# FFN and value products read their tokens alternately from two halves of a tile: pooled attention, ELU FFN and squared-ReLU FFN on one core

## The chip, the core and the metric

The kernel runs on one core of a Trainium2 chip. The metric is the device time of one execution in microseconds; the profile and its trace come from one profiled execution. PE is TensorE's matmul engine and PEld its weight loads, DVE is VectorE, ACT is ScalarE, POOL is GpSimd, and SP issues most DMAs.

## What is computed

With float32 in and out, for 2 batches of 12288 queries of 128 channels (24576 tokens in all):

```
kv_pool = kv.reshape(B, H/4, 4, W/4, 4, C).mean(axis=(2, 4))      # 768 keys per batch
k = v = kv_pool.reshape(B, 768, C) @ w_sr
a = softmax(q @ k.T / sqrt(C));   x = a @ v                       # 24576 x 128
h = x @ w_in1  (128 -> 2048);     g = where(h > 0, h, exp(min(h, 0)) - 1);   y = g @ w_out1
h = relu(y @ w_in2);              out = (h * h) @ w_out2          # 24576 x 128
```

## The kernel before

**Tiles.** Tokens go in 48 blocks `t` of 512; channels or FFN features lie on the 128 partitions, tokens along the free dimension, in every stage from the attention's values on. An FFN has 16 chunks `i` of 128 features. For each block, the attention makes scores for four groups of 128 queries (L688 to L690), row maximum, exponential, normalisation, and turned probabilities; a move by DMA finishes their transposition, and `values` (L806 to L811) makes x with tokens in the columns. Blocks 0 to 2 (`EARLY`, `PLAIN`) make their values in another way, at L833, by full fp32 matmuls.

**Products in parts.** For accuracy each float32 operand is kept as a high and a low part in fp32r (names end in H and L), and `products` (L306 to L310) makes three matmuls of one: low weight by high data, high weight by high data, high weight by low data. Each has 128 weights columns and a moving operand of 512 columns, one PSUM bank. So a block has 16 `hidden` products for each FFN (L875), 16 `down` products for each (L942), and 6 of values: 70 products of three matmuls, 210 in all, and 24 matmuls for the scores (half with 512 columns, half with 256). The last block's `down` of the second FFN runs in two halves of 256 tokens.

**Between the products.** For the ELU (`elu`, L884): `exp` on ACT, `less_one` on POOL, `pick` on DVE (tile `g`), then per pair of chunks `aH` on ACT (tile `gH`) and `aL` on DVE (tile `gL`). For the squared ReLU (`relu2`, L917): `relu` and `square` on ACT (tile `r`), `aH` on POOL (tile `sH`), `aL` on DVE (tile `sL`). `split` makes the two parts of x and y from PSUM. `store` (L965) transposes the result in 32 x 32 squares on DVE (tile `o`) and writes it with four DMAs, one for each 32 channels.

**What sets the order.** Every operation is entered in a `Program` with its engine, a cost in ns, a due time, what it comes after, and the buffers that it takes. `Program.order` (L92) runs a model of the five engines once, when the kernel is built: each engine takes the ready operation that is due first, with a little patience. Costs are multiplied by a factor `SLACK` per engine after the first 130 us. A table `MOVED` shifts the due times of single operations by hand, most of them in the opening (keys `(chunk)` or `(FFN, block, chunk)`). The result is one fixed order on each engine; every engine then works through its own in order and waits on semaphores. In the opening, PE is kept busy with matmuls on an identity (`fill`).

Of the kernel before, what the change touches and what calls it, by code (L numbers as in the profile page):

```python
# [22 lines left out]
IDLE, MARGIN, FILLER, COLD, WARM = 330.0, 60.0, 224.0, 430.0, 6300.0  # L23
OPENING, EAGER = 60000.0, 250.0
BULK = 130000.0
SLACK = {"pe": 1.0, "act": 1.17, "dve": 1.1, "pool": 1.16, "sp": 1.0}
LATENCY = {"pe": 197, "act": 135, "dve": 110, "pool": 120, "sp": 2300}
SAME = {"pe": 0, "act": 110, "dve": 0, "pool": 60, "sp": 2300}
BEGIN = {"pe": 1360.0, "act": 2500.0, "dve": 900.0, "pool": 1300.0, "sp": 1800.0}

MOVED = {
    "aH": {(0, 0, 3): 3720, (0, 2, 6): 28360, (1, 1, 5): 1580},
    "aL": {(0, 2, 2): 200, (0, 3, 1): 22430, (1, 1, 3): 2340},
    "cut": {(0, 0, 1): 12280, (0, 1, 1): 18660, (1, 1, 3): 17420},
    "down": {(0, 0, 10): -7210, (0, 0, 11): -61170, (0, 0, 9): -390, (0, 1, 11): 1860, (0, 2, 3): 17140,
        (0, 2, 9): 14060, (0, 3, 0): 4990, (0, 3, 8): -7760, (1, 0, 0): -34230, (1, 0, 11): 8280, (1, 0, 2): -28660,
        (1, 1, 2): 360, (1, 1, 3): -12810},
    "exp": {(0, 5): 9510, (0, 6): 7700, (1, 14): 10480, (2, 1): 1790, (3, 12): 55960, (3, 13): 8500},
    "hidden": {(0, 0, 12): -20, (0, 0, 8): 6730, (0, 1, 13): -3490, (0, 1, 15): -360, (0, 1, 6): 7080,
# [6 lines left out]
    "high_part": {(0, 1, 0): 11700, (1, 1, 2): 20980, (1, 1, 3): 9580},  # L46
    "join": {(1, 0, 2): -10420, (1, 1, 3): -28280},
    "k_hi": {(0, 1): -90},
    "less_one": {(3, 10): -10910, (3, 14): 17140},
    "low_part": {(1, 0, 1): 18510},  # L50
    "normalise": {(3, 0): 520, (4, 2): 4360},
    "pick": {(1, 11): 12410, (2, 0): 18920, (2, 3): -14380, (2, 6): -13180, (3, 10): -8840},
    "q_transpose": {(2,): -3420},
    "recip": {(3, 3): -2180},
    "relu": {(0, 3): -10730, (0, 7): -410, (1, 15): 11630, (1, 6): -29110, (2, 8): -3270},
    "scores": {(3, 1): 4220, (4, 3): -3470},
    "turn": {(4, 1): 11280},
    "v_hi": {(0,): 24340},
    "values": {(1, 3): -13460, (2, 1): 18540, (2, 3): 7470, (3, 2): 15850},
    "xL": {(3,): -2040},  # L60
    "yH": {(3,): -19030},
}


class Program:
# [18 lines left out]
    def op(self, name, engine, cost, priority, fn, after=(), takes=(), last=(), port=False):  # L84
        assert name not in self.ops, name
        if port:
            self.port.add(name)
        self.ops[name] = (engine, cost, priority, fn, tuple(after), tuple(takes))
        for key in last:
            self.readers.setdefault(key, set()).add(name)  # L90

    def order(self, kinds, fill=None):  # L92

        for tag, moved in MOVED.items():
            for key, by in moved.items():
                engine, cost, priority, *rest = self.ops[(tag, *key)]
                self.ops[(tag, *key)] = (engine, cost, priority + by, *rest)
# [77 lines left out]
def kernel(  # L175
# [19 lines left out]
    nc = tc.nc  # L195
# [104 lines left out]
    def buf(*key):  # L300
        return live[key]

    def f32(t):
        return t.bitcast(F32)

    def products(dst, lhs, rhs, start=True, stop=True):  # L306

        nc.tensor.matmul(dst, lhs[1], rhs[0], start=start, stop=False)  # L308
        nc.tensor.matmul(dst, lhs[0], rhs[0], start=False, stop=False)  # L309
        nc.tensor.matmul(dst, lhs[0], rhs[1], start=False, stop=stop)  # L310
# [295 lines left out]
    G = P // 32  # L606
    q_rows = q.rearrange("b (t g j) c -> (b t) j g c", g=NB // 32, j=32)
    q_tokens = q.rearrange("b (t s p) c -> (b t) p s c", s=NS, p=P)
    out_rows = out.rearrange("(t g j) c -> t j g c", g=NB // 32, j=32)

    def pieces(x, a):
        return x[32 * a:32 * (a + 1), :].rearrange("p (g i) -> p g i", i=32)
# [11 lines left out]
    def parts(tag, *t):  # L624
        return buf(tag + "H", *t), buf(tag + "L", *t)

    def attention(t, base):
# [168 lines left out]
        def weigh(j, due):  # L796
            k = (t, j)
            c0 = slice(2 * j, 2 * j + 2)

            def p_hi():  # L800
                nc.scalar.copy(buf("pH", t)[:, c0, :], f32(buf("pL", t))[:, c0, :])

            def p_lo():
                x = buf("pL", t)[:, c0, :]
                nc.vector.tensor_sub(x, f32(x), f32(buf("pH", t)[:, c0, :]))

            def values():
                vH, vL = buf("vH", b), buf("vL", b)
                for i in range(2 * j, 2 * j + 2):
                    products(buf("xps", t), (v_chunk(vH, i), v_chunk(vL, i)),  # L810
                             [buf(x, t)[:, i, :] for x in ("pH", "pL")], start=(i == 0), stop=(i == NKC - 1))  # L811

            if t >= EARLY:
                op(("p_hi", *k), "act", 945, due, p_hi, [("move", t)] + ([("p_hi", t, 0)] if j else []),
                   () if j else [("turned", ("pH", t))])
                op(("p_lo", *k), "dve", 1142, due, p_lo, [("p_hi", *k)], port=True)
            done = []
            if j == NKC // 2 - 1:
                done = [("pH", t), ("pL", t)]
                if t % BPB == BPB - 1:  # L820
                    done += [("vH", b), ("vL", b)]
            op(("values", *k), "pe", 1364, due, values,
               ([("p_lo", *k)] if t >= EARLY else [("p_lo", t, s) for s in range(NS)])
               + ([("v_lo", b)] if b == 0 else [("v_lo", b, 0), ("v_lo", b, 1)]) + ([("values", t, j - 1)] if j else []),
               [("bank" if t > 2 else "bank0", ("xps", t))] if j == 0 else (), last=done)
# [49 lines left out]
    def hidden(j, t, i, due):  # L875
        k = (j, t, i)
        x = "xy"[j]

        def fn():
            products(buf("h", *k), [w[:, i, :] for w in wi[j]], parts(x, t))  # L880

        op(("hidden", *k), "pe", 682, due, fn, [(x + "L", t), ("low_part", j, 0, i // 4)], [("bank" if t + j > 2 else "bank0", ("h", *k))],
           last=[(x + "H", t), (x + "L", t)])

    def elu(t, i, due):
# [57 lines left out]
    def down(j, t, i, due):  # L943
        pair = (j, t, i // 2)

        def fn():
            products(buf("acc", j, t), [w[:, i, :] for w in wo[j]], [buf(x, *pair)[:, i % 2, :] for x in ("aH", "aL")],
                     start=(i == 0), stop=(i == NF - 1))

        def half(h):  # L950
            x = slice(h * NB // 2, (h + 1) * NB // 2)
            products(buf("acc", j, t, h)[:, :NB // 2], [w[:, i, :] for w in wo[j]],
                     [buf(y, *pair)[:, i % 2, x] for y in ("aH", "aL")], start=(i == 0), stop=(i == NF - 1))

        after = [("aL", *pair), ("low_part", j, 1, i // 4)]
        if t == NBLK - 1 and j:
            for h in range(2):
                op(("down", j, t, i, h), "pe", 357, due + (8 * h * T if i > NF - 3 else 0), partial(half, h),
                   after + ([("down", j, t, i - 1, h)] if i else []),
                   () if i else [("bank", ("acc", j, t, h))], last=[("aH", *pair), ("aL", *pair)])  # L960
            return
        op(("down", j, t, i), "pe", 682, due, fn, after + ([("down", j, t, i - 1)] if i else []),
           () if i else [("bank" if t + j > 2 else "bank0", ("acc", j, t))], last=[("aH", *pair), ("aL", *pair)])

    def store(t, due):  # L965
# [3 lines left out]
            nc.vector.transpose(out=buf("o", t), in_=buf(*acc))  # L969

        def write():
            for a in range(G):
                queue = nc.scalar if t == NBLK - 1 and a % 2 else nc.sync
                queue.dma_start(out=out_rows[t, :, :, 32 * a:32 * (a + 1)], in_=pieces(buf("o", t), a))
# [15 lines left out]
                op(("o_write", t, h), "sp", 1000, due, partial(write_half, h), [("o_transpose", t, h)], last=[("o", t)])  # L990
            return
        op(("o_transpose", t), "dve", 630, due, transpose, [("down", 1, t, NF - 1)], [("o", ("o", t))], last=[acc])
        op(("o_write", t), "sp", 2000, due, write, [("o_transpose", t)], last=[("o", t)])


    for t in range(NKC):
# [72 lines left out]
```

## Time and profile before

| | us |
|---|---|
| median of 3 runs | 2542.16 (2542.04 to 2542.49) |
| profiled execution, its own time | 2542.52 |
| its span, first to last instruction | 2540.7 |
| PE busy | 2531.9 |
| DVE busy | 2231.3 |
| ACT busy | 2080.5 |
| POOL busy | 1308.0 |

Busy times are of the span. Matmuls overlap, and a record of one matmul of 512 columns lasts some 390 ns where the next starts about 227 ns later; so what a matmul costs is read from the starts, not from its duration, and "PE busy" does not tell how well PE is used.

### The profile page before, as it was taken

The numbers are of one execution on the slowest core, as the hardware profiler recorded it, in microseconds if no ns is written. First come the engines' busy times: TensorE is split into PE (matmuls) and PEld (weight loads), VectorE is DVE, ScalarE is ACT, GpSimd is POOL, SyncE is SP. The second block draws the span as 40 slices with busy tenths as digits, with TensorE's granted clock in tenths as the row PEclk, the third lists the DMA queues.
The fourth block names the chain that finished last, engine by engine and source line by source line (L and its number), as shares of the span: only waits on it lengthen the run. The fifth ranks groups of instructions, "written<-read, shape, count | busy, mean of one in ns | idle before, by whom it ended". The sixth has DMA issues, their size and how long they took to land.

```text
span 2540.7 us, 34933 instructions
## 1 busy us (share of the span) xinstructions
PE 2531.9 (100%) x11639; PEld 2107.5 (83%) x11639; DVE 2231.3 (88%) x2725; ACT 2080.5 (82%) x3137; POOL 1308.0 (51%) x1319
## 2 busy tenths in 40 slices
PE   9999999999999999999999999999999999999999
PEld 8888888888888888888888888888888888888888
DVE  7988889889898898988898888888888989888885
ACT  6988888788888788787888888888888888888886
POOL 4654454555665455554545445554555444544553
PEclk9999999999999999999999999999999999999999
DMA  6122111222122221221112111121112111211110
GB/s 225 38 48 49 34 38 34 55 59 46 42 46 61 56 46 42 63 51 34 38 34 56 41 38 34 45 51 34 38 34 60 37 38 34 49 44 31 33 30 13
DMA packets 358853, 119.28 MB, mean 47 GB/s; under 512 B 208912, under 2 KB 352912, under 8 KB 358672
## 3 DMA queue, kind: packets, MB, share of 16 engines
q1 hardware_dynamic: 357440, 116.85, 19.2%
q8 instruction: 92, 1.51, 0.2%
q14 instruction: 89, 0.73, 0.1%
q10 hardware_dynamic: 1232, 0.20, 0.0%
HBM read 33.61 MB, written 12.58 MB: 18 GB/s over the span
## 4 chain that ended last, share of the span: by engine, by line
PE 98%; DVE 1%; DMA 0%; ACT 0%; issue 0%; SPq 0%; DVEq 0%
PE banks L308 30%; PE banks L309 30%; PE banks L310 30%; PE banks L690 3%; PE banks L689 3%; PE banks L688 3%; PE banks L833 0%; DMA gH<-in_kv_dram 0%; PE banks L462 0%; DVE sL L933 0%; PE banks L736 0%; DVE gL L905 0%; DVE g L898 0%; DVE max L707 0%; PE banks L548 0%
## 5 line engine op out<-in xcount | busy, mean ns | idle before, releaser
L894 POOL TENSOR_SCALAR e<-e 128x512 f32<-128x512 f32 x768 | 706.4, 928 | 528.9 <-ACT e L891 441.3
L929 POOL TENSOR_SCALAR sH<-r 128x1024 fp32r<-128x1024 f32 x380 | 420.0, 1105 | 628.5 <-ACT r L926 256.3
L891 ACT ACTIVATE e<-banks 128x512 f32<-128x512 f32 x768 | 459.1, 600 | 196.7 <-PE banks L310 180.3
L933 DVE TENSOR_TENSOR sL<-r,sH 128x1024 fp32r<-128x1024 f32 x380 | 550.7, 1449 | 59.5 <-POOL sH L929 59.4
L905 DVE TENSOR_TENSOR gL<-g,gH 128x1024 fp32r<-128x1024 f32 x384 | 518.2, 1351 | 77.3 <-ACT gH L902 74.4
L923 ACT ACTIVATE r<-banks 128x512 f32<-128x512 f32 x768 | 458.9, 599 | 113.9 <-PE banks L310 98.8
L898 DVE SCALAR_TENSOR_TENSOR g<-e,banks 128x512 f32<-128x512 f32 x768 | 501.3, 671 | 24.0 <-POOL e L894 20.8
L902 ACT CAST gH<-g 128x1024 fp32r<-128x1024 f32 x384 | 401.9, 1047 | 14.2 <-DVE g L898 10.5
L926 ACT ACTIVATE r<-r 128x1024 f32<-128x1024 f32 x384 | 407.7, 1062 | 6.9
L308 PE MATMUL banks<-yH,wi1L 128*128 128x512 f32 x768 | 300.1, 391 | 0.2
L308 PE MATMUL banks<-xH,wi0L 128*128 128x512 f32 x768 | 300.1, 391 | 0.0
L308 PE MATMUL banks<-gH,wo0L 128*128 128x512 f32 x768 | 299.7, 390 | 0.0
L309 PE MATMUL banks<-yH,wi1H 128*128 128x512 f32 x768 | 299.4, 390 | 0.0
L309 PE MATMUL banks<-gH,wo0H 128*128 128x512 f32 x768 | 299.4, 390 | 0.0
L309 PE MATMUL banks<-xH,wi0H 128*128 128x512 f32 x768 | 299.2, 390 | 0.0
L310 PE MATMUL banks<-xL,wi0H 128*128 128x512 f32 x768 | 298.9, 389 | 0.0
L310 PE MATMUL banks<-yL,wi1H 128*128 128x512 f32 x768 | 298.8, 389 | 0.0
L310 PE MATMUL banks<-gL,wo0H 128*128 128x512 f32 x768 | 298.8, 389 | 0.0
L310 PE MATMUL banks<-sL,wo1H 128*128 128x512 f32 (+1 forms) x768 | 297.4, 387 | 1.0 <-DVE sL L933 1.0
L308 PE MATMUL banks<-sH,wo1L 128*128 128x512 f32 (+1 forms) x768 | 297.8, 388 | 0.0
L309 PE MATMUL banks<-sH,wo1H 128*128 128x512 f32 (+1 forms) x768 | 297.4, 387 | 0.0
L711 ACT ACTIVATE prob<-banks,max 128x768 f32<-128x768 f32 x191 | 172.3, 902 | 49.5 <-DVE max L707 46.4
(181 smaller groups left out, 4327.9 us busy)
## 6 DMA issues: line engine op xcount, KB each, us to landing
pL<-turned SPq DMA_DIRECT2D x720, 96.0 KB, 2.2
out_dram<-o SPq DMA_DIRECT2D x188, 64.0 KB, 1.9
q<-in_q_dram SPq DMA_DIRECT2D x180, 64.0 KB, 2.3
ld<-in_kv_dram SPq DMA_DIRECT2D x24, 256.0 KB, 3.6
ld<-in_kv_dram SPq DMA_DIRECT2D x4, 512.0 KB, 5.5
g<-in_kv_dram SPq DMA_DIRECT2D x4, 512.0 KB, 6.3
gH<-in_kv_dram SPq DMA_DIRECT2D x3, 512.0 KB, 7.8
r<-in_moe_w_in_dram SPq DMA_DIRECT2D x3, 511.8 KB, 6.9
```

Source lines behind the costliest of these rows:

```text
L308: nc.tensor.matmul(dst, lhs[1], rhs[0], start=start, stop=False)
L309: nc.tensor.matmul(dst, lhs[0], rhs[0], start=False, stop=False)
L310: nc.tensor.matmul(dst, lhs[0], rhs[1], start=False, stop=stop)
L891: nc.scalar.activation(buf("e", *k), buf(*h), AF.Exp)
L894: nc.gpsimd.tensor_scalar(out=buf("e", *k), in0=buf("e", *k), scalar1=-1.0, scalar2=1.0, op0=ALU.add, op1=ALU.mult)
L898: nc.vector.scalar_tensor_tensor(out=buf("g", *pair)[:, i % 2, :], in0=buf("e", *k), scalar=0.0, in1=buf(*h), op0=ALU.min, op1=ALU.max)
L902: nc.scalar.copy(buf("aH", 0, *pair), buf("g", *pair))
L905: nc.vector.tensor_sub(buf("aL", 0, *pair), buf("g", *pair), f32(buf("aH", 0, *pair)))
L923: nc.scalar.activation(buf("r", *pair)[:, i % 2, :], buf(*h), AF.Relu)
L926: nc.scalar.activation(buf("r", *pair), buf("r", *pair), AF.Square)
L929: nc.gpsimd.tensor_scalar(out=buf("aH", 1, *pair), in0=buf("r", *pair), scalar1=1.0, scalar2=1.0, op0=ALU.mult, op1=ALU.mult)
L933: nc.vector.tensor_sub(buf("aL", 1, *pair), buf("r", *pair), f32(buf("aH", 1, *pair)))
```

## The change

- Wherever x, y, the probabilities or the activations are the moving operand of a `products` call (`values`, `hidden`, `down`), the 512 columns are now read through `paired`: a view of the tile as two halves of 256, of which one column is taken from each in turn (0, 256, 1, 257, ...). The result's columns stand in that order. The scores, whose moving operands are the keys, and the values of blocks 0 to 2 are as before.
- From values to the end a block of 3 or later is turned five times, blocks 0 to 2 four times. The stores put the results to the rows that belong to them: `out_rows` has its two factors exchanged, and blocks 0 to 2 are written with eight DMAs in place of four.
- The planner's costs of the turned products are 648 for 682 and 1296 for 1364, and its factors for DVE and POOL 1.085 and 1.09 for 1.1 and 1.16. A new table `AFTER` shifts the due times of whole kinds of operation from block 3 on, and `MOVED` is another table (of both one entry is shown).

```diff
-SLACK = {"pe": 1.0, "act": 1.17, "dve": 1.1, "pool": 1.16, "sp": 1.0}
+SLACK = {"pe": 1.0, "act": 1.17, "dve": 1.085, "pool": 1.09, "sp": 1.0}
...
+AFTER = {("aH", 1): 8560, ("aL", 0): 1530, ("aL", 1): -9360, ("down", 1): -1890, "exp": -5170,
...
-    "aH": {(0, 0, 3): 3720, (0, 2, 6): 28360, (1, 1, 5): 1580},
+    "aH": {(1, 1, 0): 12060, (1, 1, 1): 5250},
...
     def order(self, kinds, fill=None):
 
+        for name, (engine, cost, priority, *rest) in self.ops.items():
+            if priority > -9e5 and len(name) <= 4:
+                staged = name[0] in ("hidden", "down", "aH", "aL")
+                block = name[1 + staged] if len(name) > 1 + staged else 0
+                if block >= 3:
+                    priority += AFTER.get(name[:2] if staged else name[0], 0)
+                    self.ops[name] = (engine, cost, priority, *rest)
...
+    def paired(x):
+        return x.rearrange("p (a b) -> p b a", a=2)
...
-    out_rows = out.rearrange("(t g j) c -> t j g c", g=NB // 32, j=32)
+    out_rows = out.rearrange("(t j g) c -> t j g c", g=NB // 32, j=32)
+    out_early = out.rearrange("(t k g e) c -> t e k g c", g=NB // 32, k=16, e=2)
...
-                             [buf(x, t)[:, i, :] for x in ("pH", "pL")], start=(i == 0), stop=(i == NKC - 1))
+                             [paired(buf(x, t)[:, i, :]) for x in ("pH", "pL")], start=(i == 0), stop=(i == NKC - 1))
...
-            op(("values", *k), "pe", 1364, due, values,
+            op(("values", *k), "pe", 1296, due, values,
...
-            products(buf("h", *k), [w[:, i, :] for w in wi[j]], parts(x, t))
-
-        op(("hidden", *k), "pe", 682, due, fn, [(x + "L", t), ("low_part", j, 0, i // 4)], [("bank" if t + j > 2 else "bank0", ("h", *k))],
+            products(buf("h", *k), [w[:, i, :] for w in wi[j]], [paired(y) for y in parts(x, t)])
+
+        op(("hidden", *k), "pe", 648, due, fn, [(x + "L", t), ("low_part", j, 0, i // 4)], [("bank" if t + j > 2 else "bank0", ("h", *k))],
...
-            products(buf("acc", j, t), [w[:, i, :] for w in wo[j]], [buf(x, *pair)[:, i % 2, :] for x in ("aH", "aL")],
+            products(buf("acc", j, t), [w[:, i, :] for w in wo[j]], [paired(buf(x, *pair)[:, i % 2, :]) for x in ("aH", "aL")],
                      start=(i == 0), stop=(i == NF - 1))
 
         def half(h):
-            x = slice(h * NB // 2, (h + 1) * NB // 2)
+            x = slice(h * NB // 4, (h + 1) * NB // 4)
             products(buf("acc", j, t, h)[:, :NB // 2], [w[:, i, :] for w in wo[j]],
-                     [buf(y, *pair)[:, i % 2, x] for y in ("aH", "aL")], start=(i == 0), stop=(i == NF - 1))
+                     [paired(buf(y, *pair)[:, i % 2, :])[:, x, :] for y in ("aH", "aL")], start=(i == 0), stop=(i == NF - 1))
...
-        op(("down", j, t, i), "pe", 682, due, fn, after + ([("down", j, t, i - 1)] if i else []),
+        op(("down", j, t, i), "pe", 648, due, fn, after + ([("down", j, t, i - 1)] if i else []),
...
+            if t < PLAIN:
+                for a in range(G):
+                    for e in range(2):
+                        nc.sync.dma_start(out=out_early[t, e, :, :, 32 * a:32 * (a + 1)],
+                                          in_=pieces(buf("o", t), a)[16 * e:16 * (e + 1)])
+                return
...
-        op(("o_write", t), "sp", 2000, due, write, [("o_transpose", t)], last=[("o", t)])
+        op(("o_write", t), "sp", 4000 if t < PLAIN else 2000, due, write, [("o_transpose", t)], last=[("o", t)])
```

The new tables put the operations of all engines in another order. Two places show it, both at chunk 4 of block 11's second FFN. On DVE, before, the operations ahead of that chunk's `sL` (L933) are these; `max`, `sum` and `rcp` belong to the softmax, `turned` is the transpose of probabilities, the numbers behind names tell tiles apart:

```order
L933 TENSOR_TENSOR sL_6784<-r_6700,sH_6749 128x1024
L717 TENSOR_SCALAR sum_6773<-sum_6773 128x1
L718 RECIPROCAL rcp_6794<-sum_6773 128x1
L707 TENSOR_REDUCE max_6814<-banks 128x1
L898 SCALAR_TENSOR_TENSOR g_6751<-e_6763,banks 128x512
L729 STREAM_TRANSPOSE turned_6688<-prob_6729 128x24x32
L898 SCALAR_TENSOR_TENSOR g_6838<-e_6789,banks 128x512
L898 SCALAR_TENSOR_TENSOR g_6838<-e_6808,banks 128x512
L717 TENSOR_SCALAR sum_6825<-sum_6825 128x1
L718 RECIPROCAL rcp_6852<-sum_6825 128x1
L707 TENSOR_REDUCE max_6859<-banks 128x1
L905 TENSOR_TENSOR gL_6865<-g_6751,gH_6833 128x1024
```

The next row is `sL_6877`, with `gL_6881` behind it. Now these stand there, and the last row is the same chunk's `sL` (now L949):

```order
L723 TENSOR_REDUCE max_6795<-banks 128x1
L914 SCALAR_TENSOR_TENSOR g_6803<-e_6779,banks 128x512
L745 STREAM_TRANSPOSE turned_6811<-prob_6625 128x24x32
L914 SCALAR_TENSOR_TENSOR g_6803<-e_6798,banks 128x512
L733 TENSOR_SCALAR sum_6805<-sum_6805 128x1
L734 RECIPROCAL rcp_6833<-sum_6805 128x1
L745 STREAM_TRANSPOSE turned_6811<-prob_6691 128x24x32
L723 TENSOR_REDUCE max_6845<-banks 128x1
L914 SCALAR_TENSOR_TENSOR g_6850<-e_6816,banks 128x512
L745 STREAM_TRANSPOSE turned_6811<-prob_6750 128x24x32
L949 TENSOR_TENSOR sL_6868<-r_6748,sH_6824 128x1024
```

Three transposes of one block's probabilities stand close together ahead of `sL` where one stood, and `gL` has moved behind it.

On PE, at the same chunk, before: the second product of the pair follows the first at once.

```order
L308 MATMUL banks<-yH_6409,wi1L 128x512
L309 MATMUL banks<-yH_6409,wi1H 128x512
L310 MATMUL banks<-yL_6420,wi1H 128x512
L308 MATMUL banks<-sH_6797,wo1L 128x512
L309 MATMUL banks<-sH_6797,wo1H 128x512
L310 MATMUL banks<-sL_6877,wo1H 128x512
L308 MATMUL banks<-sH_6797,wo1L 128x512
L309 MATMUL banks<-sH_6797,wo1H 128x512
L310 MATMUL banks<-sL_6877,wo1H 128x512
```

Now products of the first FFN and a hidden product come behind the first of the pair:

```order
L323 MATMUL banks<-xH_6719,wi0L 128x512
L324 MATMUL banks<-xH_6719,wi0H 128x512
L325 MATMUL banks<-xL_6759,wi0H 128x512
L323 MATMUL banks<-sH_6824,wo1L 128x512
L324 MATMUL banks<-sH_6824,wo1H 128x512
L325 MATMUL banks<-sL_6868,wo1H 128x512
L323 MATMUL banks<-gH_6836,wo0L 128x512
L324 MATMUL banks<-gH_6836,wo0H 128x512
L325 MATMUL banks<-gL_6878,wo0H 128x512
```

Each product is still three matmuls of 128x512, and a block's count of them is unchanged.

## Rows read from the trace of the kernel before

**Rows 1.** The page: span, engines, clock in 40 slices, chain, and one group.

```profile
span 2540.7 us, 34933 instructions
...
PE 2531.9 (100%) x11639; PEld 2107.5 (83%) x11639; DVE 2231.3 (88%) x2725; ACT 2080.5 (82%) x3137; POOL 1308.0 (51%) x1319
...
PEclk9999999999999999999999999999999999999999
...
PE 98%; DVE 1%; DMA 0%; ACT 0%; issue 0%; SPq 0%; DVEq 0%
PE banks L308 30%; PE banks L309 30%; PE banks L310 30%; PE banks L690 3%; PE banks L689 3%; PE banks L688 3%; PE banks L833 0%; DMA gH<-in_kv_dram 0%; PE banks L462 0%; DVE sL L933 0%; PE banks L736 0%; DVE gL L905 0%; DVE g L898 0%; DVE max L707 0%; PE banks L548 0%
...
L933 DVE TENSOR_TENSOR sL<-r,sH 128x1024 fp32r<-128x1024 f32 x380 | 550.7, 1449 | 59.5 <-POOL sH L929 59.4
```

**Rows 2.** PE's timeline: start us, duration us, engine, line, operation, shapes.

```profile
999.70 0.39 PE L308 MATMUL banks<-sH,wo1L 128*128 128x512 f32 x1
...
1003.78 0.39 PE L688 MATMUL banks<-kH,qTH 128*128 128x512 f32 x1
...
1004.46 0.28 PE L688 MATMUL banks<-kH,qTH 128*128 128x256 f32 x1
1004.57 0.28 PE L689 MATMUL banks<-kL,qTH 128*128 128x256 f32 x1
1004.69 0.28 PE L690 MATMUL banks<-kH,qTL 128*128 128x256 f32 x1
1004.81 0.40 PE L308 MATMUL banks<-yH,wi1L 128*128 128x512 f32 x1
```

**Rows 3.** Busy time by stretch: its length, then PE, PEld, DVE, ACT, POOL, clock.

```profile
0.00:40.00 40.00, 37.45 (x268) 33.76 (x269) 23.75 (x56) 21.11 (x44) 8.38 (x13) 1.00 0.89 326
40.00:130.00 90.00, 88.64 (x477) 75.07 (x476) 82.93 (x119) 83.58 (x141) 62.03 (x65) 1.00 0.16 41
...
520.00:1150.00 630.00, 628.90 (x2833) 520.05 (x2832) 561.19 (x679) 515.31 (x778) 356.94 (x355) 1.00 0.21 50
...
1300.00:2400.00 1100.00, 1100.00 (x4966) 914.40 (x4965) 982.18 (x1190) 908.57 (x1359) 546.76 (x551) 1.00 0.18 40
```

**Rows 4.** Waits: engine and line, released by; us in total, times, longest.

```profile
PE banks L310 <- DVE sL L933: 1.0, 1, 1.0
...
DVE gL L905 <- ACT gH L902: 74.4, 122, 1.7
DVE sL L933 <- POOL sH L929: 59.4, 59, 1.8
```

**Rows 5.** Groups of PE's matmuls: counts behind the shapes; busy us, mean ns.

```profile
L308 PE MATMUL banks<-yH,wi1L 128*128 128x512 f32 x768 | 300.1, 391 | 0.2
...
L308 PE MATMUL banks<-sH,wo1L 128*128 128x512 f32 (+1 forms) x768 | 297.8, 388 | 0.0
...
L308 PE MATMUL banks<-turned,vL 128*128 128x512 f32 x270 | 105.8, 392 | 0.0
```

**Rows 6.** Timeline around PE's late product, 697 to 700 us, DVE and PE.

```profile
697.67 2.07 DVE L933 TENSOR_TENSOR sL<-r,sH 128x1024 fp32r<-128x1024 f32 x1
...
698.44 0.39 PE L309 MATMUL banks<-sH,wo1H 128*128 128x512 f32 x1
699.80 0.50 PE L310 MATMUL banks<-sL,wo1H 128*128 128x512 f32 x1 [0.97 <-DVE sL L933]
```

**Rows 7.** Matmuls of line 308 alone in the first 130 us, columns as in rows 3.

```profile
0.00:130.00 130.00, 38.18 (x97) 18.30 (x97) 1.00 0.39 129
```

**Rows 8.** Stores: issues and landing (us); issue durations (ns); the last two matmuls.

```profile
out_dram<-o SPq DMA_DIRECT2D x188, 64.0 KB, 1.9
...
L974 SPq DMA_DIRECT2D out_dram<-o x188: 315/489/2168, 161.3 to 2520.1; - x188
...
2536.46 0.28 PE L309 MATMUL banks<-sH,wo1H 128*128 128x256 f32 x1
2536.58 0.28 PE L310 MATMUL banks<-sL,wo1H 128*128 128x256 f32 x1
```

More of the change, by code (lines that the diff above doesn't have):

```diff
@@ L29 @@
 BEGIN = {"pe": 1360.0, "act": 2500.0, "dve": 900.0, "pool": 1300.0, "sp": 1800.0}
+AFTER = {("aH", 1): 8560, ("aL", 0): 1530, ("aL", 1): -9360, ("down", 1): -1890, "exp": -5170,
+         ("hidden", 0): 520, ("hidden", 1): 500, "less_one": 4410, "o_transpose": -5280, "p_hi": 10050,
+         "p_lo": -1040, "pick": -2620, "recip": -3590, "scores": -6800, "turn": 25890, "xL": 7740}
 MOVED = {
-    "aH": {(0, 0, 3): 3720, (0, 2, 6): 28360, (1, 1, 5): 1580},
-    "aL": {(0, 2, 2): 200, (0, 3, 1): 22430, (1, 1, 3): 2340},
@@ L34 @@
[L34 to L39, printed above, removed]
[6 rows of a table removed]
@@ L46 @@
[L46 to L61, printed above, removed]
+    "aH": {(1, 1, 0): 12060, (1, 1, 1): 5250},
+    "aL": {(0, 2, 5): 14860, (0, 3, 7): 2230, (0, 4, 1): -15440, (1, 1, 0): 7790, (1, 1, 2): 8410},
+    "cut": {(0, 1, 0): -41650},
+    "down": {(0, 1, 10): 360, (0, 1, 11): 3120, (0, 1, 7): -21830, (0, 1, 9): -34650, (0, 2, 0): -11550,
+        (0, 2, 12): -10550, (0, 2, 15): -19040, (0, 2, 4): 2060, (0, 3, 8): 73460, (1, 0, 1): -10000,
+        (1, 0, 11): -7140, (1, 0, 15): -10410, (1, 0, 3): -10890, (1, 0, 6): -24480, (1, 1, 0): 2660,
+        (1, 1, 2): 5540},
@@ new lines @@
+    "exp": {(3, 13): -29550, (3, 15): -1510},
+    "exps": {(2, 0): -39560, (4, 3): 45250, (5, 3): 22370},
+    "fold": {(1, 0, 2): 8060},
+    "hidden": {(0, 1, 1): -5070, (0, 1, 12): 5960, (0, 1, 15): 6630, (0, 2, 1): 1740, (0, 2, 10): 4140,
[7 rows of a table added]
+    "join": {(0, 1, 2): 7160, (0, 1, 3): -16850},
+    "k_lo": {(0, 0): 23080},
+    "less_one": {(0, 7): -9610, (1, 8): 2630, (3, 9): -27910, (4, 1): -11320},
+    "low_part": {(0, 1, 3): 24890},
+    "normalise": {(1, 0): 42460, (3, 0): 4950},
+    "p_hi": {(3, 0): -4080, (4, 1): 5000, (4, 2): 670},
@@ new lines @@
+    "p_lo": {(4, 2): -16470},
+    "pick": {(1, 0): 41710, (2, 15): 13160, (3, 15): -12810, (3, 5): 34510, (4, 5): -12910},
+    "recip": {(2, 1): 3250, (3, 2): 3020, (4, 2): 23200},
+    "relu": {(0, 1): -4570, (1, 0): -14160, (1, 1): -8810, (1, 2): 4410, (2, 2): -15030, (2, 7): 11550},
+    "scores": {(2, 0): -2380, (3, 0): 3090, (4, 2): 7970, (4, 3): 8200, (5, 3): 24570},
+    "square": {(0, 4): 4000, (2, 1): -33900},
+    "v_hi": {(0,): -2040},
+    "values": {(1, 0): -5220, (2, 0): 2940},
@@ L62 @@
+    "yL": {(2,): -14940},
 }
```

13 rows, old and new, of the table MOVED are left out of this document.

## The prediction

> **What bounds the kernel now.** I read the page first. [...] PE's busy share alone proves little, since its matmuls overlap. So the next view is PE's timeline, start to start [rows 2]. Between 999.70 and 1003.78 us stand 18 matmuls of 512 columns, without a pause: 4.08 / 18 = 226.7 ns each. Those of 256 columns start at 1004.46, 1004.57, 1004.69, and the next one at 1004.81: 0.11, then 0.12 and 0.12 us. The first step is half of 227, so what a matmul costs goes with its columns, and is no fixed toll per matmul; the later 0.12 may be held by the weight load, whose records I did not need here.
>
> The third view is the table by stage [rows 3]. From 1300 to 2400 us PE started 4966 matmuls in 1100 us. One block has 234: 192 of the two FFNs and 18 of the values, with 512 columns, and 24 of the scores, half of 512 and half of 256. That is 4966/234 = 21.22 blocks of 51.83 us. Taking 12 x 0.117 = 1.41 us for the short ones (0.35 us per three [rows 2]) leaves 50.42 / 222 = 227.1 ns for a matmul of 512 columns: there is no idle time in the block, PE's streaming is the whole of it. In the same stage DVE works 982.2/21.22 = 46.3 us per block, ACT 42.8, GpSimd (POOL) 25.8.
>
> The fourth view is the waits [rows 4]. PE's own come to 1.0 us for the one late DVE result in the steady part. It is seen in the timeline [rows 6]: `sL` came late, and the matmul that reads it starts at 699.80, 1.36 us after the one at 698.44, where 0.23 is usual, so 1.1 us were lost. DVE itself waits in small pieces, for `gH` of ACT (74.4 us in sum) and `sH` of POOL (59.4), and has 309 us of idle time in all.
>
> **The change, part by part.**
>
> *The moving operand.* Nothing is added or removed on PE: the same matmuls with the same weights, but 512 columns are now read as 0, 256, 1, 257 and so on. The matmuls that change (the rows show line 308, one of each three) [rows 5]: hidden 2 x 768 x 3 = 4608; down of the ELU FFN 768 x 3 = 2304; down of the ReLU² FFN 752 x 3 = 2256 (the last block's 16 steps run in halves of 256 columns); values 270 x 3 = 810. Sum 9978 with 512 columns. The 96 half matmuls (16 x 2 x 3) come 0.12 us apart [rows 8] like the short scores, and I let them stay there; if they fell to 0.11, that is 1 us.
>
> What an alternating read costs no row shows: all moving operands of the kernel before are contiguous. [...] The one number that speaks for a value is in the code: the planner's cost for three such matmuls was 682 = 3 x 227.3, which is what the rows give, and its cost for six score matmuls, 1070, is near the 1.03 us of [rows 2]; its new cost for the three is 648 = 3 x 216, and for six values 1296, the same. PE costs of this table have followed the chip so far. So 227.1 - 216 = 11.1 ns, times 9978 = -110.8 us.
>
> [...]
>
> *What is late next.* At 216 ns a block takes 51.83 - 210 x 0.0111 = 49.50 us on PE. DVE's 46.3 us of work are then 93.5% of it, ACT's 42.8 are 86%, POOL's 25.8 are 52%. DVE's idle time per block shrinks from 5.5 to 3.2 us, and much of that idle time is waiting in an order fixed beforehand, not spare time. The order is new everywhere (due times, and a smaller factor for DVE and POOL in the planner). Ahead of the `sL` that was late in the trace at 698 us, DVE's order now has three transposes `turned` close together, where one stood. The stage from 520 to 1150 us is the tightest: POOL does the second batch's keys there (356.9/630 busy against 546.8/1100 later), and the late product lies in it, behind an `sL` subtraction of 2.07 us, where 1449 ns is the mean [rows 1, 6]. Bounds of what PE will wait: from 0 to DVE as the bound, priced below at 44 us. I take 6 us, some five times today's 1.1, nearer to the low end, since from 40 to 130 us, with DVE at 92%, PE was without a matmul for 1.4 us [rows 3].
>
> *The opening.* Up to 130 us DVE and ACT are full (82.9 and 83.6 of 90 us from 40 to 130 [rows 3]). Line 308, one of each three, has 97 matmuls there [rows 7], so at most 291 of the changed ones, worth 3.2 us; I count half and some as lost: +2 us. Its new table moves weight loads between buffers and adds three filler matmuls; I take 0, between -4 and +4, as PE was without a matmul for 2.5 + 1.4 = 3.9 us there.
>
> *Stores.* The turned rows change which rows a store writes, not its bytes: still 4 DMAs of 64 KB per block, 1.9 us to landing [rows 8], with 50 us until the buffer is wanted. The first three blocks issue 8 instead of 4: 12 more issues of about 489 ns on SP's queue [rows 8], with loads of later blocks behind them that are due a block later. I cost them at nothing; without cover it is 2 us per block, 6 in all. The end of the kernel, 4.1 us from the start of the last matmul at 2536.58 [rows 8] to the end of the span, stays.
>
> *Sum,* against the profiled execution's 2542.5 us (0.4 above the median of the runs): 2542.5 - 110.8 + 6 + 2 = 2439.7, rounded to 2440.
>
> **The rivals.**
>
> *DVE becomes the bound.* For it: 93.5% of a block, and the share it reached over the fullest long stretch is 82.9/90 = 92.1% [rows 3]; PE already waited once at 89%. Against it: no row has DVE held back by itself alone, and from 40 to 130 us its load had the opening's chains in it. At 92.1% a block takes 46.3/0.921 = 50.3 us, 0.8 over PE's 49.5; for 45 blocks 36 us, and with the tightest stage's 12 blocks waiting some 0.7 us more, 44 us: 2476.
>
> *The matmul stays at 227 ns.* [...] Against it: the half-price step of 0.11 us, which lies in the reading. All that is left then is the new order: 2542, between 2535 and 2550.
>
> [...]
> [...]
>
> [...]
>
> **How the numbers follow.** Forecast (2428 to 2455): 0.70. DVE bound: 0.19. Half the excess: 0.03. No change of the matmul: 0.04. Slower: 0.04. What a measurement of this kernel can tell from no change is 0.2%, 5 us. Faster has the first three, 0.92; of the no-change case 0.03 falls within 5 us and 0.01 is given to slower, with the 0.04: same 0.03, slower 0.05. The range runs from 2425 (no waits, the opening 4 us shorter, and a little of a matmul below 216 ns) to 2485 (above the DVE case); it leaves out the last two cases and a little on either end.
>
> **What would show it.** In the profile after: 512-column matmuls of FFN and values start 0.216 us apart, those of the scores (contiguous as before) still 0.227; a block from 1300 us on has 234 matmuls in about 49.5 us; DVE's share rises to 92 or 93%, its work per block stays near 46.3 us; PE waits for `sL` or `gL` add up to some 6 us, most between 500 and 1100 us. The prediction is wrong if the FFN matmuls still start 0.227 apart or more, or if PE's waits for DVE pass 20 us.

## The result, and the profile after

The changed kernel takes 2430.36 us (median; 2429.91 to 2430.43) where the one before takes 2542.1: 0.956 of it, 95% interval 0.9543 to 0.9576, 111.7 us less. The forecast was 2440, in a range of 2425 to 2485. (One correction to the description of the inputs above: the four FFN weight matrices arrive as float64, whose bits the kernel takes apart itself; no step rests on it.)

From the page of the profile after: span, engines, clock, chain by engine.

```profile
span 2428.0 us, 34913 instructions
...
PE 2420.1 (100%) x11645; PEld 2124.4 (87%) x11645; DVE 2164.9 (89%) x2725; ACT 2076.5 (86%) x3137; POOL 1305.5 (54%) x1319
...
PEclk9999999999999999999999999999999999999999
...
PE 98%; DVE 1%; ACT 1%; DMA 0%; issue 0%; POOL 0%; SPq 0%; DVEq 0%; ACTq 0%
```

PE is 98% of the chain, as before [rows 1]. DVE's busy time fell by 66 us, though it does the same work; that is a finding of its own, below.

PE's timeline after (start us, duration us): a product, the scores twelve matmuls later, and the product behind them:

```profile
1399.96 0.38 PE L323 MATMUL banks<-gH,wo0L 128*128 128x512 f32 x1
...
1402.55 0.40 PE L704 MATMUL banks<-kH,qTH 128*128 128x512 f32 x1
...
1403.24 0.28 PE L704 MATMUL banks<-kH,qTH 128*128 128x256 f32 x1
...
1403.59 0.38 PE L323 MATMUL banks<-xH,wi0L 128*128 128x512 f32 x1
```

From 1399.96 to 1402.55 are 12 alternating matmuls: 215.8 ns each, against 226.7 in [rows 2]. The scores, still contiguous, take 0.23.

Busy time by stretch, as in [rows 3] (length, then PE, PEld, DVE, ACT, POOL, clock):

```profile
0.00:40.00 40.00, 38.17 (x274) 35.19 (x275) 24.71 (x56) 21.57 (x45) 9.23 (x13) 1.00 0.91 329
40.00:130.00 90.00, 88.13 (x484) 75.78 (x483) 84.42 (x121) 84.31 (x142) 63.76 (x66) 1.00 0.15 39
...
500.00:1100.00 600.00, 600.00 (x2841) 526.24 (x2840) 551.16 (x680) 519.94 (x781) 336.70 (x357) 1.00 0.23 53
...
1300.00:2280.00 980.00, 980.00 (x4632) 859.62 (x4631) 877.03 (x1109) 844.46 (x1269) 533.70 (x516) 1.00 0.19 43
```

From 1300 us on, 4632 / 234 = 19.79 blocks stand in 980 us, 49.5 us each, as forecast. DVE's work is 877.0 / 19.79 = 44.3 us per block, not 46.3: 89.5%, as before (982.2 / 1100 = 89.3% [rows 3]). From 500 to 1100 us PE is never without a matmul.

The waits after, as in [rows 4], and the group of the subtraction `sL`, as in [rows 1]:

```profile
PE banks L656 <- DVE g L914: 0.7, 1, 0.7
PE banks L323 <- DVE g L914: 0.4, 2, 0.2
...
DVE sL L949 <- POOL sH L945: 45.1, 91, 2.7
```

```profile
L949 DVE TENSOR_TENSOR sL<-r,sH 128x1024 fp32r<-128x1024 f32 x380 | 496.9, 1308 | 45.3 <-POOL sH L945 45.1
```

PE's wait for `sL` is gone, and its other waits lie in the opening. The mean `sL` fell from 1449 to 1308 ns.

### The profile page after: what moved, and what is told of

Same layout as the page of the kernel before. It is cut to its first block, busy times and chain, and to the rows that moved or that the text cites. A ratio compares the mean times of both kernels' runs of the same rounds, so it can differ in the third digit from the quotient of the medians.

```text
span 2428.0 us, 34913 instructions
## 1 busy us (share of the span) xinstructions
PE 2420.1 (100%) x11645; PEld 2124.4 (87%) x11645; DVE 2164.9 (89%) x2725; ACT 2076.5 (86%) x3137; POOL 1305.5 (54%) x1319
## 4 chain that ended last, share of the span: by engine, by line
PE 98%; DVE 1%; ACT 1%; DMA 0%; issue 0%; POOL 0%; SPq 0%; DVEq 0%; ACTq 0%
PE banks L323 29%; PE banks L324 29%; PE banks L325 29%; PE banks L704 3%; PE banks L706 3%; PE banks L705 3%; PE banks L849 0%; DMA gH<-in_kv_dram 0%; DVE g L914 0%; PE banks L477 0%; DVE gL L921 0%; DVE yH L369 0%; ACT e L907 0%; PE banks L752 0%; PE banks L563 0%
## 5 line engine op out<-in xcount | busy, mean ns | idle before, releaser
L910 POOL TENSOR_SCALAR e<-e 128x512 f32<-128x512 f32 x768 | 745.6, 975 | 674.0 <-ACT e L907 662.1
L945 POOL TENSOR_SCALAR sH<-r 128x1024 fp32r<-128x1024 f32 x380 | 402.8, 1060 | 374.8 <-PE banks L324 108.1
L949 DVE TENSOR_TENSOR sL<-r,sH 128x1024 fp32r<-128x1024 f32 x380 | 496.9, 1308 | 45.3 <-POOL sH L945 45.1
L323 PE MATMUL banks<-xH,wi0L 128*128 128x512 f32 x768 | 292.0, 380 | 0.2 <-DVE g L914 0.2
L323 PE MATMUL banks<-yH,wi1L 128*128 128x512 f32 x768 | 291.6, 380 | 0.0
L324 PE MATMUL banks<-yH,wi1H 128*128 128x512 f32 x768 | 291.4, 379 | 0.0
L324 PE MATMUL banks<-xH,wi0H 128*128 128x512 f32 x768 | 291.4, 379 | 0.0
L324 PE MATMUL banks<-gH,wo0H 128*128 128x512 f32 x768 | 291.4, 379 | 0.0
L323 PE MATMUL banks<-sH,wo1L 128*128 128x512 f32 (+1 forms) x768 | 289.8, 377 | 0.0
L723 DVE TENSOR_REDUCE max<-banks 128x1 f32<-128x768 f32 x188 | 177.7, 945 | 28.8 <-PE banks L706 28.6
```

Source lines behind the costliest of these rows:

```text
L910: nc.gpsimd.tensor_scalar(out=buf("e", *k), in0=buf("e", *k), scalar1=-1.0, scalar2=1.0, op0=ALU.add, op1=ALU.mult)
L945: nc.gpsimd.tensor_scalar(out=buf("aH", 1, *pair), in0=buf("r", *pair), scalar1=1.0, scalar2=1.0, op0=ALU.mult, op1=ALU.mult)
L949: nc.vector.tensor_sub(buf("aL", 1, *pair), buf("r", *pair), f32(buf("aH", 1, *pair)))
```

## The experiments

### The reading without the order, and the order without the reading

`e1_reading_alone` is the kernel before with `paired` and the turned stores, and nothing of the planner changed; `e2_order_alone` is the kernel after without them.

```diff
 e1, against the kernel before
+    def paired(x):
+        return x.rearrange("p (a b) -> p b a", a=2)
...
+            products(buf("h", *k), [w[:, i, :] for w in wi[j]], [paired(y) for y in parts(x, t)])
 e2, against the kernel after
-        return x.rearrange("p (a b) -> p b a", a=2)
+        return x
```

> The order of before, word for word on every engine, with the alternating reads and the turned stores alone. Theory A (the whole gain is the read: 9978 matmuls x 11.2 ns = 112 us, and the order is not needed for it): 2430 to 2436, PE waits under 5 us. Rival B (the old order cannot feed PE at 216 ns: DVE has 46.3 us of work in a block of 49.5, with subtractions sL of 1.45 us on the mean): matmuls start 0.216 apart too, but PE waits for sL and gL by 0.5 to 1 us per block, 2455 to 2480.

> The order of the changed kernel, with contiguous reads and the old stores. Theory A: the order gives PE nothing, matmuls are 0.227 apart, 2540 to 2546. Rival B (the order itself frees PE): below 2535. Either way the mean of the sL subtraction tells whether its fall from 1449 to 1308 ns comes from the order (then about 1310 here) or from the reads (then about 1450).

Measured: e1 2440.85 us (0.9602 of before, 0.9586 to 0.9618), e2 2539.63 (0.9991, 0.9981 to 1.0). So the reading alone is worth 101.1 us, the order alone 2.3, and both together 111.6: the order is worth 2.3 us to a PE at 227 ns and 10.5 to one at 216. The 2.3 us are small: no run of e2 (2539.27 to 2540.15) reaches one of the kernel before (2541.77 to 2542.47), but the interval ends at no change. For e1 neither theory held in full: 5 us over the upper end of A, and far below B.

Where e1 loses most of the 10.5 us shows in its stretches, and in part in PE's waits:

```profile
500.00:1100.00 600.00, 596.75 (x2799) 516.44 (x2798) 550.67 (x671) 506.44 (x769) 352.33 (x352) 1.00 0.22 53
...
1300.00:2280.00 980.00, 980.00 (x4632) 859.33 (x4631) 903.19 (x1111) 843.50 (x1269) 513.74 (x515) 1.00 0.18 42
```

```profile
PE banks L313 <- DVE sL L937: 1.9, 2, 1.1
...
PE banks L311 <- ACT r L927: 1.1, 3, 0.4
```

From 1300 us on the old order feeds PE just as well, 4632 matmuls in 980 us. In the stage with the second batch's keys it starts 2799 where the new order starts 2841: 42 x 0.216 = 9 us. Both late subtractions lie there; the waits view names less than 3 us of it, and the rest is in many smaller delays: the steps from start to start in that stage, so far as they are over 25 ns longer than is usual for their width, are too long by 8.6 us in sum in e1, and by 0.4 in the kernel after. That is the stage that the prediction named.

The subtraction `sL` in the stretch from 200 to 2300 us, in e1 and in e2:

```profile
L937 DVE TENSOR_TENSOR sL<-r,sH 128x1024 fp32r<-128x1024 f32 x338 | 491.0, 1453 | 23.3 <-POOL sH L933 23.1
```

```profile
L949 DVE TENSOR_TENSOR sL<-r,sH 128x1024 fp32r<-128x1024 f32 x323 | 425.9, 1318 | 28.2 <-POOL sH L945 28.0
```

1453 ns in the old order with the new reading, 1318 in the new order with the old one: the shorter subtractions come from the order. In the same stretch, from the start and length of each instruction, a `sL` with next to no POOL instruction beside it (whose lengths are rough) takes 1.21 to 1.22 us on the mean in all four kernels (before, e1, e2, after); that is 58 of 323 before and 141 of 323 in e2, and the others take 1.52 us before and 1.40 in e2. So fewer subtractions beside POOL fit the fall, but no run separates that; nor was tried which of the new tables (factors, due times by kind, single due times) it is.

e2's steady stretch gives DVE's work per block in the new order with the old reading:

```profile
1300.00:2280.00 980.00, 980.00 (x4425) 815.02 (x4425) 853.00 (x1060) 808.99 (x1212) 473.15 (x494) 1.00 0.18 41
```

853.0 / (4425 / 234) = 45.1 us, against 46.3 before, 903.2 / 19.79 = 45.6 in e1 and 44.3 with both. So the order alone takes 1.2 of the 2.0 us, the reading alone 0.7.

### Which patterns are fast

`e3_patterns` and `e9_lines` run 48 matmuls of each pattern with idle engines, `e4_patterns_busy` some of them beside ACT, DVE and POOL at work. Their core, where `a`, `b`, `n` and `r` count columns:

```python
halves(a): x[:, :512].rearrange("p (a b) -> p b a", a=a)         # 0, 512/a, 2*512/a, ..., 1, ...
near(d):   x[:, :512].rearrange("p (n a b) -> p n b a", a=2, b=d)  # 0, d, 1, d+1, ...
runs(r):   x[:, :512].rearrange("p (a n r) -> p n a r", a=2, r=r)  # r columns of each half in turn
```

What do the 11 ns between contiguous (227) and alternating (216) hang on? A1: on the pattern alone, so that four or eight places are as good as two. A2: on the other engines' reads and writes, so that contiguous takes 216 too where they stand still. C: on where the other half lies.

> Only runs of 48 matmuls of one stationary tile, each run with another way to read the moving columns, while all other engines stand still; nothing of the reference is computed. [...] Rival C (it is a matter of where the other half lies): only some distances give 0.216. Halves of 128 pairs: 0.111 against 0.120 for 256 contiguous columns. Contiguous bf16: 0.216.

> Ten of the same runs while ACT copies, DVE subtracts and POOL multiplies tiles of 1024 columns all the time; nothing of the reference is computed. Theory A1: the same starts as with idle engines, within 1 ns. Theory A2: contiguous 0.227 here and 0.216 with idle engines, halves 0.216 in both.

> Runs of 48 matmuls only, other engines idle; nothing of the reference is computed. What does alternating need: theory A3, two neighbours in the order must lie in different groups of four columns (16 bytes): then a distance of 3 columns is part good (some of its pairs share a group), a distance of 4 that starts at column 2 is good as at column 0, and halves are good from column 2 too. For bf16 (2 bytes a column) contiguous is 216 already; a distance of 8 columns is 16 bytes, and A3 gives 216, a distance of 4 no more than that. Rival (any alternation of 4-byte columns is good, and bf16 suffers from it at any distance, as from halves: 484): bf16 at 8 near 480.

The timeline of e3: the time of a pattern is the step from its start to the next one's, over 48. In order: contiguous, halves, quarters, eighths, sixteenths; a distance of 2 and of 4 columns, and what follows; runs of 2, and what follows; with 256 columns contiguous and halves, and what follows; bf16 contiguous, bf16 halves. The granted clock is 1.00 from 20 to 400 us.

```profile
20.35 11.04 PE L64 MATMUL banks<-x,w 128*128 128x512 f32 x48
31.23 10.52 PE L66 MATMUL banks<-x,w 128*128 128x512 f32 x48
41.59 13.75 PE L68 MATMUL banks<-x,w 128*128 128x512 f32 x48
55.17 23.56 PE L70 MATMUL banks<-x,w 128*128 128x512 f32 x48
78.53 21.08 PE L72 MATMUL banks<-x,w 128*128 128x512 f32 x48
...
164.03 11.09 PE L80 MATMUL banks<-x,w 128*128 128x512 f32 x48
174.96 10.52 PE L82 MATMUL banks<-x,w 128*128 128x512 f32 x48
185.32 10.52 PE L84 MATMUL banks<-x,w 128*128 128x512 f32 x48
...
237.12 16.48 PE L94 MATMUL banks<-x,w 128*128 128x512 f32 x48
253.43 12.18 PE L96 MATMUL banks<-x,w 128*128 128x512 f32 x48
...
353.80 5.92 PE L110 MATMUL banks<-x,w 128*128 128x256 f32 x48
359.56 5.52 PE L112 MATMUL banks<-x,w 128*128 128x256 f32 x48
364.92 5.48 PE L114 MATMUL banks<-x,w 128*128 128x128 f32 x48
...
386.56 10.53 PE L120 MATMUL banks<-y,wb 128*128 128x512 bf16 x48
396.93 23.41 PE L122 MATMUL banks<-y,wb 128*128 128x512 bf16 x48
```

Contiguous takes (31.23 - 20.35) / 48 = 227 ns with nothing else running, halves 216, quarters 283, eighths 487, every second column 453. A distance of 2 columns stays at 228, one of 4 gives 216 like halves; runs of two columns from each half take 340.

In e4, beside busy engines (contiguous, halves, quarters, and what follows; from 21 to 56 us DVE is busy for 34.4, ACT for 34.0 and POOL for 33.5 of 35 us):

```profile
21.23 11.04 PE L75 MATMUL banks<-x,w 128*128 128x512 f32 x48
32.12 10.52 PE L77 MATMUL banks<-x,w 128*128 128x512 f32 x48
42.47 13.75 PE L79 MATMUL banks<-x,w 128*128 128x512 f32 x48
56.05 10.53 PE L81 MATMUL banks<-x,w 128*128 128x512 f32 x48
```

The steps are 227, 216 and 283 ns again. So the 11 ns are no quarrel with other engines (A2 falls), they belong to the pattern. But A1 was too simple: alternating between two places takes 216 ns, between four 67 ns more.

In e9 (from column 2: contiguous, then halves, and a distance of 4; then with 384 columns a distance of 3, and what follows, halves and contiguous; bf16 at a distance of 8, and of 4, which ends at 142.29):

```profile
32.07 11.37 PE L66 MATMUL banks<-x,w 128*128 128x512 f32 x48
43.28 10.52 PE L68 MATMUL banks<-x,w 128*128 128x512 f32 x48
53.64 10.56 PE L70 MATMUL banks<-x,w 128*128 128x512 f32 x48
64.04 11.04 PE L72 MATMUL banks<-x,w 128*128 128x512 f32 x48
74.92 9.92 PE L74 MATMUL banks<-x,w 128*128 128x384 f32 x48
84.68 7.97 PE L76 MATMUL banks<-x,w 128*128 128x384 f32 x48
92.48 7.96 PE L78 MATMUL banks<-x,w 128*128 128x384 f32 x48
100.28 8.50 PE L80 MATMUL banks<-x,w 128*128 128x384 f32 x48
108.62 23.48 PE L82 MATMUL banks<-y,wb 128*128 128x512 bf16 x48
131.93 10.52 PE L84 MATMUL banks<-y,wb 128*128 128x512 bf16 x48
```

(L68 is halves from column 0 again, as a measure.) Contiguous from column 2 takes 234 ns, halves from there 217, but the distance of 4 from there 227; from column 0 it is 216. (That row is no blow to A3: from column 2 the order runs 2, 6, 3, 7, 4, 8, and by A3 7 and 4 share a group of four, so it did not promise 216; the expectation did.) A distance of 3 takes 203 ns for 384 columns, where contiguous takes 174. For bf16 a distance of 8 columns takes 486 and one of 4 takes 216, the reverse of A3. A3 fits the 4-byte columns in part (in e3 a distance of 2 takes 228 ns and one of 4 takes 216) and fails for bf16. No run shows its groups of four, so the mechanism stays open; what is shown is the table of patterns.

The widths show one thing more, which the prediction had otherwise. Contiguous, 384 columns take (108.62 - 100.28) / 48 = 174 ns, in halves (100.28 - 92.48) / 48 = 162.5: 11 ns between them, the same as with 512 columns. In e3, 256 columns take 120 ns contiguous and 112 in halves (which something else may hold up, as 128 columns take 111 and 112). A price that goes with the columns would have made the contiguous ones 170 and 113. So what alternating saves here is a sum per matmul, some 11 ns, the same at 384 as at 512 columns.

### Four places in the kernel itself

```diff
-        return x.rearrange("p (a b) -> p b a", a=2)
+        return x.rearrange("p (a b) -> p b a", a=4)
```

> The changed kernel with the same operands read from four quarters in turn (0, 128, 256, 384, 1, ...); the stores are not adapted to it, so results stand in other rows. Theory A (two places at a time are free, four are not; from the pattern runs 282.9 ns against 215.8): 2430 + 9978 x 67.1 = 2430 + 670 = 3100, the halves of the last block aside. [...] If the kernel's traffic hid the pattern: 2430 to 2500.

Measured: 3094.69 us, a single run. The first of three matmuls in a row, and the scores behind them:

```profile
1399.75 0.45 PE L323 MATMUL banks<-gH,wo0L 128*128 128x512 f32 x1
...
1400.60 0.39 PE L704 MATMUL banks<-kH,qTH 128*128 128x512 f32 x1
```

0.85 / 3 = 0.283 us per matmul, as in the pattern runs: their table prices the kernel within 6 us of 670. So a slower kernel was no idle chance (0.04 in the prediction); two halves happen to be on the good side. How often the reading changes its place does not set the price: two places and four both change it at every column, and take 216 and 283 ns.

### Is DVE the next bound?

```diff
+                if t >= EARLY:
+                    nc.vector.tensor_reduce(out=spare, in_=buf("prob", *k)[:, :NB], op=ALU.max, axis=AX.X)
                 nc.vector.tensor_scalar_add(buf("sum", *k), buf("sum", *k), EPS)
```

> The changed kernel, with one more DVE instruction ahead of each of the four reciprocals of a block (a maximum over 512 columns of the probabilities into a spare number, some 0.65 us each); the order is unchanged otherwise. DVE's work in a block of the steady part goes from 44.3 to some 46.9 us, 95% of PE's 49.5. Theory A (DVE's share alone costs nothing, since PE's buffers are filled ahead; only the order at single places does): PE waits under 10 us more, 2430 to 2440. The rival of the prediction (DVE binds from a share of about 92%): 46.9/0.921 = 50.9 us a block, 2490 to 2500.

Measured: 2433.42 us, 3.1 more than the changed kernel. Its steady stretch, and the added instructions from 1300 to 2280 us:

```profile
1300.00:2280.00 980.00, 980.00 (x4633) 857.94 (x4632) 929.67 (x1190) 842.93 (x1269) 556.66 (x516) 1.00 0.19 43
```

```profile
L735 DVE TENSOR_REDUCE spare<-prob 128x1 f32<-128x512 f32 x80 | 54.1, 676 | 0.0
```

DVE is busy for 929.7 / 980 = 94.9%, and PE starts as many matmuls as in the changed kernel. The rival of a bound at 92% falls; theory A holds.

### The scores read alternately too

The keys are written turned, once per batch, and their matmuls read them through `paired`, so that the scores come out in the old order; in `e7_scores_too_planned` the planner is told.

```diff
+            kept_as = paired if x == "k" else (lambda keys: keys)
...
-                nc.scalar.activation(buf(*hi)[:, x], flat(buf(*ps))[:, x], AF.Copy, scale=scale)
+                nc.scalar.activation(kept_as(buf(*hi)[:, x]), flat(buf(*ps))[:, x], AF.Copy, scale=scale)
...
-                    nc.tensor.matmul(ps[:, y], x[0], kH[:, y], start=True, stop=False)
+                    nc.tensor.matmul(ps[:, y], x[0], paired(kH[:, y]), start=True, stop=False)
...
-                op(("scores", *k), "pe", 1070, due, scores,
+                op(("scores", *k), "pe", 984 if t >= EARLY else 1070, due, scores,        # e7 alone
```

> The changed kernel, with the keys stored turned, so that the scores' matmuls of block 1 on read them alternately too; planner's costs and order unchanged. Theory A (a matmul reading alternately takes 216 ns, 111.5 with 256 columns, whatever it is for): per block 12 x (232 - 216) + 12 x (117.3 - 111.5) = 262 ns, 12 us over 47 blocks: 2417 to 2420. Rival (the scores are slower in the changed kernel for another reason, waits for their banks or for the queries): no gain, 2430.

> As the run before, with the planner's cost of a group of six score matmuls from block 3 on at 984 instead of 1070, so that the order is planned anew with the old tables of due times. Theory A: the same 2417 to 2420, give or take the 10 us that an order was seen to be worth; the tables were made for the other cost, so rather worse than better: 2418 to 2430. Rival: 2430 or more.

Measured: e6 2419.45 us (0.9517 of before, 0.9503 to 0.9531), 10.9 below the changed kernel; e7 2423.07. The scores in e6:

```profile
1403.42 0.38 PE L705 MATMUL banks<-kH,qTH 128*128 128x512 f32 x1
...
1404.07 0.27 PE L705 MATMUL banks<-kH,qTH 128*128 128x256 f32 x1
...
1404.40 0.38 PE L323 MATMUL banks<-yH,wi1L 128*128 128x512 f32 x1
```

Six of them take 0.98 us, where the changed kernel takes 1.04. With the better cost the plan is 3.6 us worse: counted like those of e1, from 130 us on, the long steps between PE's starts come to 4.5 us in e7 and to 0.9 in e6. That the due times were made for the other cost is the likely reason, and is not shown. e6 is the fastest kernel here.

## Why the prediction was right

- *The bound* was PE's streaming, and it still is: PE is 98% of the chain before and after, and is busy for 980.0 of 980 us from 1300 to 2280.
- *The operand*: 216 ns taken, 215.8 measured. 9978 x (227.1 - 215.8) = 113 us, and 2542.5 - 113 = 2429.5, where the profiled execution of the kernel after took 2429.9. The term was right, and its reason was not: the value, which no row of before shows, was taken from the planner's cost, and that is what came true. The step of 0.11 us in [rows 2] was read as "goes with its columns, and is no fixed toll per matmul", and weighed against a matmul that stays at 227. It is the one short step beside two of 0.12, behind a matmul of 512 columns; in a run of its own width a contiguous matmul of 256 takes 120 ns, and the 11 ns that go are the same at 384 and at 512 columns. They are a fixed sum per matmul that goes with the reading nonetheless. In that the forecast had luck; and nothing in the rows told the sign, as the quarters show.
- *What is late next* was mis-sized, by the 6 us that PE does not wait. Two numbers failed. DVE's work per block was carried over as 46.3 us, and it is 44.3, of which the order alone takes 1.2 us (e2); so DVE's share did not rise to 92 or 93% but stayed at 89.5. And the three transposes ahead of `sL` were read as a danger from the order alone, where PE has no gap now. With the old order the forecast would have been right to a microsecond (2440 against 2440.85 in e1), but by luck: the reading gives 113 us, not 110.8, and 11 us are lost on the way, not 8. Most of the 11 us do lie in the stage that was named; the working described a kernel without its new plan.
- *DVE as the bound* (0.19) was given too much: at 94.9% it costs 3 us (e5).
- *The opening*: to 130 us PE runs 12 matmuls more than before. Six of them are fillers (matmuls on the identity: 38 for 32, not three more); 6 x 0.22 = 1.3 of 3.2 us were gained, so 1.9 were lost, where 2 were counted.
- *The stores* cost nothing that shows. *The half matmuls* went from 120 to 112 ns, 1 us, as left open.
- *Half the excess* (0.03) and *slower* (0.04) were the author's estimates: all moving operands of the kernel before are contiguous, so none of its rows shows how much of the 227 ns can go, or what a change of place costs. Measured, two places take 216 ns, four 283 and eight 487 (e3).

## What to carry over

Read the cost of a matmul from start to start, in runs of one width, and compare widths and patterns before naming what a difference goes with: here it was the same 11 ns at 384 and at 512 columns, and it still lay in the operand's access pattern, which can be changed without touching the work. Try such a pattern by itself first, in a run that takes half a millisecond, since patterns that look alike here differ by a factor of two (bf16 at a distance of 4 and of 8 columns: 216 and 486 ns). A plan made for the new speed was worth 10.5 us on the faster PE and 2.3 on the slow one: time it with the change, and again when costs move.

## What the hardware showed beyond expectation

With 512 columns, one fp32r matmul takes 227 ns contiguous (in e3, at a granted clock of 1.00), 216 alternating between two places (from column 0, at every distance tried from 4 columns to half of the tile), and 283 between four, with every other engine idle as with them busy (two places then at 16, 32 and 256 columns); between eight it takes 487 (tried with idle engines alone). The 11 ns between contiguous and halves are the same with 384 columns (174 and 162.5). For bf16 halves are the slow ones: 216 contiguous, 484 between halves, and 216 or 486 at a distance of 4 or 8 columns. And contiguous fp32r from column 2 takes 234.
